# General code placed ahead of the main code, and 192-token tails stored in eight or nine transfers

## The chip, the core and the metric

The kernel runs on one core of a Trainium2 chip. The metric is the device time of one execution in microseconds (us). Times inside an execution are counted from the start of its profiled span. The profile names the engines PE (matrix products), DVE (vector), ACT (scalar), POOL (GpSimd) and SP (sync); the granted clock is the share of full clock speed that PE was allowed.

A run is called slow when it is over 1.5% above the fastest run of the same kernel.

## The reference, cut to what matters

```python
B, N, m, C = 4, 12480, 32, 128            # x: 4 x 12480 x 128, inducing: 32 x 128
def mab(q, kv):                            # attention of q over kv
    s = scale * (q @ kv.T); a = softmax(s); return a @ kv
h = mab(inducing, x)                       # per batch: 32 x 128
y = mab(x, h)                              # 4 x 12480 x 128
out = gelu(y @ w_in) @ w_out               # 128 -> 2048 -> 128, all float32 outside
```

Both inputs and outputs are large against the arithmetic: 25.6 MB of tokens are read and 25.6 MB are written. Each batch of 12480 tokens is cut into six units of 2048 tokens and a tail of 192. The kernel uses a short form of the second part that holds for small values, checks on the chip that it was allowed to, and otherwise runs a slow general code.

## The kernel before, where the change touches it

A pair of full units lies on 128 partitions and is stored in one transfer of 2 MB. The tail lies on 96 partitions with 1 KB each and is stored in one transfer of 96 KB. In the last batch each unit (1 MB) is stored alone. All stores, the first load and the inducing points are issued by the sync engine (SP); all other loads, which convert to 16 bits on the way, by GpSimd (POOL). Data is moved by 16 DMA engines, called rings here; a transfer is spread over up to 16 of them. The packet records do not name a ring, so "a ring ends" means one of the 16 last data packets, or completions, of a transfer.

```python
x_first = sb.tile([128, 32, 128], FP32, tag="o", bufs=OBUFS)
...
nc.sync.dma_start(out=x_first[:, :16, :], in_=src[:, :16, :])     # first unit, as fp32
nc.gpsimd.dma_start(out=x_pair[:, 16:, :], in_=src[:, 16:, :])    # bulk loads follow
a_load(units[0][2])
...
nc.sync.dma_start(out=ind_s, in_=inducing)                        # inducing points, 16 KB
nc.tensor.transpose(indT_ps, ind_s, identity[:M, :M])             # first work of PE
...
def b_store(bt, u, alone):
    if alone:
        c0, c1, o = u.c_pair, u.c_pair + u.nc, bt.live[("o", u.idx)]
    else:
        c0, c1, o = 0, u.held, bt.live[("pair", u.pair)]
    nc.sync.dma_start(out=u.rows_of(out)[:, c0:c1, :], in_=o)
...
with tc.If(flag > 0, preferred_fallthrough_block=False):
    general(tc, x, moe_w_in, moe_w_out, out, ind_s, identity)     # the rare code
```

The instructions of each engine are issued in the written order. Completion of a transfer is counted on a semaphore, which an engine can wait for. The framework gives SP's transfers eight of them in turn (108, 109 and 113 to 118 in the issue records), and lets SP wait, before it issues a transfer, until the transfer eight back, which had the same semaphore, has landed entirely.

## Time and profile before

| | before |
|---|---|
| time | 134.17 us median (134.0 to 134.32) |
| span of the profiled execution | 132.8 us |
| rings' busy share (sum of the four queues) | 98.4%, so 2.1 us idle (packets overlap, so some 3.7 us too low) |
| first load landed (its semaphore full) | 6.1 us |
| last arithmetic | 122.9 us |
| last store's data: median ring / last ring | 128.6 / 131.2 us |

First the page of the kernel before: its span, the rows of the DMA in 40 slices of 3.3 us (a digit is the busy share in tenths, the row below it GB/s), and the shares of the two data queues (packets, MB, share of the 16 engines' span). Queue 0 carries GpSimd's loads, queue 1 SP's transfers.

```profile
span 132.8 us, 3490 instructions
...
DMA  4999999999999999999999999999999999999970
GB/s 123 302 223 215 217 200 220 212 220 210 220 205 220 215 200 313 333 398 367 299 318 348 266 227 324 321 412 425 430 423 426 415 437 413 411 434 425 421 300 15
...
q0 software_dynamic: 2848, 13.30, 49.5%
q1 hardware_dynamic: 2800, 26.63, 48.3%
```

The DMA row is what matters: from the second slice to the 38th it never falls below 9. The kernel is limited by its transfers, and idle time of the arithmetic engines costs nothing as long as this row stays full.

Then how it starts: the timeline of SP, and the first instruction of PE, with the start in us, the duration, and in brackets how long the engine was idle before it and what ended that.

```profile
0.75 0.38 SPq L285 DMA_DIRECT2D x_first<-in_x_dram  x1
1.19 0.42 SPq L295 DMA_DIRECT2D ind_s<-in_inducing_dram  x1
```

Last, the waits of SP, by what ended them (us in total, number, longest):

```profile
SPq L713 <- DVE pair L701: 90.2, 9, 42.7
SPq L713 <- POOL pair L686: 8.6, 5, 2.1
SPq L713 <- DVE o L701: 8.6, 6, 3.0
SPq L1141 <- DMA out_dram<-o: 5.9, 3, 3.3
```

At the store line (L713) SP waits for results only, never for an earlier store. Its waits for stores are at the end of the program (L1141).

### The profile page before, as it was taken

Reading aid. Unit: us, or ns where it says so; the run is one execution under the profiler, and the core shown is the slowest. Engines: PE = TensorE matmul, PEld = TensorE weight load, DVE = VectorE, ACT = ScalarE, POOL = GpSimd, SP = SyncE. Lnnn points to the kernel's source line nnn. Section 1 sums busy time; section 2 is a strip of 40 time slices with the busy share of each in tenths; the row PEclk is TensorE's granted clock in tenths of the full one; section 3 lists DMA queues with packets and bytes.
Section 4 is the critical chain, followed back from the end, with each engine's and each line's share of the span. In section 5 each row is a group of like instructions: output and inputs, shape, how many; then the busy total and the mean of one; then the engine's idle time right before and its main releaser. Section 6 shows DMA issues by size and latency. Waiting matters only on the chain. (4 is left out here: it accounts for less than half of the span.)

```text
span 132.8 us, 3490 instructions
## 1 busy us (share of the span) xinstructions
PE 97.3 (73%) x1365; PEld 56.6 (43%) x1365; DVE 93.4 (70%) x266; ACT 76.2 (57%) x173; POOL 65.3 (49%) x85
## 2 busy tenths in 40 slices
PE   0098678449999999999697979957988779295000
PEld 0036545349465556665363555624544424131000
DVE  1086557323699998999999489749989999998000
ACT  3004273316866879598878458967779759174000
POOL 6920131119344646894824409914167999556000
PEclk9999999965899999999999999999999999955555
DMA  4999999999999999999999999999999999999970
GB/s 123 302 223 215 217 200 220 212 220 210 220 205 220 215 200 313 333 398 367 299 318 348 266 227 324 321 412 425 430 423 426 415 437 413 411 434 425 421 300 15
DMA packets 5666, 40.17 MB, mean 303 GB/s; under 512 B 624, under 2 KB 1936, under 8 KB 2192
## 3 DMA queue, kind: packets, MB, share of 16 engines
q0 software_dynamic: 2848, 13.30, 49.5%
q1 hardware_dynamic: 2800, 26.63, 48.3%
q8 instruction: 11, 0.18, 0.5%
q14 instruction: 7, 0.06, 0.1%
HBM read 27.67 MB, written 25.56 MB: 401 GB/s over the span
## 5 line engine op out<-in xcount | busy, mean ns | idle before, releaser
L686 POOL TENSOR_TENSOR pair<-pair,rr 128x512 f32<-128x512 f32 x29 | 30.3, 1056 | 29.1 <-ACT pair L355 19.9
L670 PE MATMUL at<-q,e 128*128 128x512 f16 (+1 forms) x104 | 33.5, 389 | 7.2 <-DVE o L701 2.4
L367 PE MATMUL tr<-identity_h,xh 128*128 128x128 f16 x392 | 29.3, 227 | 2.3 <-DMA xh<-in_x_dram 2.1
L701 DVE TENSOR_TENSOR pair<-at,rr 128x512 f32<-128x512 f32 x41 | 26.8, 679 | 3.1 <-DMA out_dram<-pair 1.6
L367 PEld LDWEIGHTS <-xh 128*128 128x128 f16 x392 | 24.5, 102 | 7.6 <-issue 3.5
L355 ACT ACTIVATE xT<-tr 128x1024 f16<-128x1024 f16 (+1 forms) x17 | 16.7, 981 | 19.1 <-PE tr L367 19.1
L353 DVE COPY xT<-tr 128x1024 f16<-128x1024 f16 (+1 forms) x35 | 21.9, 644 | 7.0 <-PE tr L367 6.7
L355 ACT ACTIVATE pair<-at 128x512 f32<-128x512 f32 x29 | 17.2, 598 | 3.1 <-PE at L670 1.7
L628 ACT ACTIVATE e<-s 128x512 f16<-128x512 f32 (+1 forms) x28 | 15.2, 563 | 6.4 <-PE s L616 5.2
L277 POOL DMA_DIRECT2D xh<-in_x_dram x15 | 8.3, 556 | 21.5 <-DMA xh<-in_x_dram 14.3
L393 ACT ACTIVATE e<-s 128x512 f16<-128x512 f32 (+1 forms) x28 | 15.2, 543 | 5.4 <-PE s L381 5.0
L670 PEld LDWEIGHTS <-e 128*128 128x128 f16 (+1 forms) x104 | 8.9, 105 | 11.5 <-issue 8.5
L415 PE MATMUL hun<-xh,e1t 128*32 128x128 f16 x392 | 10.5, 222 | 3.2 <-DVE e1t L407 3.0
L562 POOL TENSOR_TENSOR pt<-pt 128x512 f32<-128x512 f32 (+4 forms) x20 | 12.0, 601 | 1.5
L407 DVE STREAM_TRANSPOSE e1t<-e 128x256 int32<-128x256 int32 (+1 forms) x28 | 11.0, 399 | 2.2 <-ACT e L393 2.2
L381 PE MATMUL s<-xT,indT 128*32 128x512 f16 (+1 forms) x108 | 10.5, 376 | 1.6 <-ACT xT L355 0.8
L415 PEld LDWEIGHTS <-e1t 128*32 128x32 f16 x392 | 6.3, 96 | 11.5 <-DVE e1t L407 9.0
L701 DVE TENSOR_TENSOR o<-at,rr 128x512 f32<-128x512 f32 (+1 forms) x19 | 10.2, 558 | 0.9 <-PE at L670 0.7
L686 POOL TENSOR_TENSOR o<-o,rr 128x512 f32<-128x512 f32 x8 | 8.2, 1044 | 4.0 <-ACT o L355 2.3
L616 PE MATMUL s<-xT,hT 128*32 128x512 f16 (+1 forms) x100 | 9.7, 391 | 0.1
L640 PEld LDWEIGHTS <-e 128*128 128x128 f16 (+1 forms) x104 | 5.6, 99 | 5.0 <-issue 1.3
L640 PE MATMUL r<-strand,e 128*128 128x4 f16 (+1 forms) x104 | 6.9, 168 | 0.2 <-ACT e L393 0.2
(72 smaller groups left out, 93.0 us busy)
## 6 DMA issues: line engine op xcount, KB each, us to landing
out_dram<-pair SPq DMA_DIRECT2D x9, 2048.0 KB, 15.0
xh<-in_x_dram POOLq DMA_DIRECT2D x11, 1024.0 KB, 28.0
out_dram<-o SPq DMA_DIRECT2D x6, 1024.0 KB, 7.5
x_first<-in_x_dram SPq DMA_DIRECT2D x1, 1024.0 KB, 5.4
xh<-in_x_dram POOLq DMA_DIRECT2D x1, 512.0 KB, 7.3
w_in_h<-in_moe_w_in_dram POOLq DMA_DIRECT2D x1, 512.0 KB, 17.5
w_out_h<-in_moe_w_out_dram POOLq DMA_DIRECT2D x1, 512.0 KB, 19.5
out_dram<-o SPq DMA_DIRECT2D x4, 96.0 KB, 12.4
```

Of the source, the lines that this page charges most:

```text
L353: nc.vector.tensor_copy(out=out, in_=in_)
L355: nc.scalar.activation(out=out, in_=in_, func=AF.Copy)
L367: nc.tensor.transpose(tr[:, c - c0, : u.p], xh[: u.p, c, :], identity_h[: u.p, : u.p])
L393: nc.scalar.activation(out=e1[: u.p, : u.nc // 2, :, :], in_=s1[: u.p, : u.nc, :].rearrange("r (a b) i -> r a i b", b=2), func=AF.Exp, sca ...
L407: nc.vector.transpose(out=pairs(e1t)[: u.p, :n], in_=pairs(e1)[: u.p, :n])
L415: nc.tensor.matmul(bt.hun[32 * j : 32 * j + 32, :], e1t[: u.p, c // 2, :, c % 2], xh[: u.p, c, :], start=u.idx == 0 and c < 4, stop=c + 4 ...
L562: nc.gpsimd.tensor_tensor(out=bt.pt[:, :, :, :half], in0=bt.pt[:, :, :, :half], in1=bt.pt[:, :, :, half : 2 * half], op=ALU.add,)
L628: nc.scalar.activation(out=e2[: u.rows, : u.cols], in_=s2[: u.rows, : u.cols], func=AF.Exp, scale=SCALE,)
L640: nc.tensor.matmul(r2[: u.p, ci, : u.nj], e2[: u.rows, ci * u.p : (ci + 1) * u.p], strand[: u.rows, : u.nj], start=True, stop=True,)
L670: nc.tensor.matmul(at[: u.p, : u.nj, :], e2[: u.rows, ci * u.p : (ci + 1) * u.p], bt.q[: u.rows, : u.nj, :], start=True, stop=True,)
L686: nc.gpsimd.tensor_tensor(out=part, in0=part, in1=rr2[: u.p, ci, : u.nj].unsqueeze(2).broadcast_to([u.p, u.nj, 128]), op=ALU.mult,)
L701: nc.vector.tensor_tensor(out=ov[: u.p, ci, :, :], in0=at[: u.p, : u.nj, :], in1=rr2[: u.p, ci, : u.nj].unsqueeze(2).broadcast_to([u.p, u. ...
```

## The change

It has two parts. The stores of the tails are cut so that rings with a high number get fewer of the 96 rows: the rings do not end together, and one that ends late holds up the end. In the last batch, the parts are moved behind the last large store. And the rare code is laid ahead of the main code, so that the usual path does not jump over it at the end, where instruction fetches were seen among the last stores.

```diff
+    left_over = []
     def b_store(bt, u, alone):
         ...
-        nc.sync.dma_start(out=u.rows_of(out)[:, c0:c1, :], in_=o)
+        parts = [u.p]
+        if u.tail:
+            parts = [1, 3, 5, 7, 9, 11, 13, 15, 32]
+        if u.tail and u.b == B - 1:
+            parts = [2, 4, 6, 8, 10, 12, 14, 40]
+        left_over.append((u, parts, c0, c1, o))
+        if u.tail and u.b == B - 1:
+            return
+        for u, parts, c0, c1, o in left_over[::-1] if u.b == B - 1 else left_over:
+            p0 = 0
+            for n in parts:
+                nc.sync.dma_start(
+                    out=u.rows_of(out)[p0 : p0 + n, c0:c1, :], in_=o[p0 : p0 + n]
+                )
+                p0 += n
+        left_over.clear()
@@
+    nc.at_finalize(general_first)
     return nc
+
+def general_first(nc):
+    blocks = nc.main_func.blocks
+    rare = [b for b in blocks if "_true" in b.name]
+    rest = [b for b in blocks if "_true" not in b.name]
+    nc.main_func.blocks = rest[:1] + rare + rest[1:]
```

## The prediction

> **What bounds it now.** The DMA engines. The slice table shows the DMA row at 9 (90% or more) from the second slice to the 38th. The last load lands at 88.9 us; from then on only stores run, back to back. The last arithmetic ends at 122.9 us (timeline), the last store's final completion packet starts at 131.2 us, the span ends at 132.8. In the DMA packet records the 16 rings end the last store between 127.6 and 131.2 us, median 128.6. One ring is slow (8 KB about every 316 ns instead of 306), starts the last store 1.9 us behind, and also carries an 8 KB instruction fetch at 128.5 us, with a packet after it stretched to 0.82 us. Another gets a 16 KB fetch (0.89 us). These follow the branch over the general code.
>
> **What the change intends.** The Trainium skill ("DMA: Bandwidth & Descriptors", on why a DMA increments its semaphore by 16) says that a transfer issued from SP runs on the lowest-numbered k engines, k being the largest divisor of the partition count up to 16. Parts of 1, 3, ... 15 and 32 then put 10 rows on ring 0 and 2 on ring 15 instead of 6 each (no record here names rings). A row of 1 KB takes about 42 ns, so the last ring is spared 4 rows three times and 6 once: about 0.75 us. General code first removes the jump at the end and probably the late fetches: 0.4 to 0.9 us. Alone, these would give at most 1%.
>
> **What it adds.** 31 more transfers on SP, 0.33 to 0.41 us of issue each. Worse, the issue records show SP's transfers cycling through eight semaphores, and each reuse waits until the transfer eight back has landed. The tail is issued right behind a large store (61.2, 84.8, 106.4 us), so its eighth part waits for that store to land, and SP, in order, holds all later stores. The store queue drains at each tail:
> - Batch 0: loads still fill the rings; almost free.
> - Batches 1 and 2: no loads are left. About 0.5 us until SP sees the landing (as at the end now), two part issues 0.9, issue to first packet 1.0 (as for the first load): 2.5 us empty each. The next stores' data are ready (94.4, 111.4 us), so 5 us are lost.
> - Batch 3: the eighth part waits for the very last large store. Then come its issue, SP's flag load, branch and closing waits, about 2.7 us, hidden today: about 3 us.
>
> Sum: 8 lost, less 0.75 of rows, about 0.8 of fetches, and up to 1 because an empty queue lets the late ring catch up: +5.7 us.
>
> **Predicted: 140.0 us, range 136.7 to 142.3. Faster by over 2%: 0.04; within 2%: 0.14; slower: 0.82.**
>
> **What would show it.** SP waits at the store line for DMA out_dram, many us in total, none today. GB/s dips below 300 near slices 30 and 35. The next large stores issue only near 99 to 101 and 115 to 117 us. Tail stores land last, and SP's flag load comes after 134 us. The late fetch records are gone, and the start is longer by at most 0.3 us. Without these waits the end should come at 131.5 to 132.5 us.
>
> **What would make it wrong.** Semaphores assigned otherwise than in turn; a drain costing less because the late ring sets the pace anyway; a fetch at the start, when all engines jump over the general code, delaying the first loads by 1 to 2 us.

## More of the kernel before

The kernel before takes 134 to 135 us on the chips that were used.

```profile
6.43 0.28 PE L297 MATMUL indT_ps<-identity,ind_s 32*128 32x32 f32 x1 [6.43 <-DMA ind_s<-in_inducing_dram]
```

The first load is issued at once. It has the rings to itself until 4.7 us, and PE begins at 6.4 us, when the inducing points that follow it have landed.

## The result, and the profile after

The changed kernel takes 145.11 us (144.9 to 145.43) against 134.17 us. Ratios here are the mean time of one kernel's fast runs over that of the other's of the same rounds, so not quite the ratio of the medians that are quoted. This one is 1.082, with a 95% interval of 1.079 to 1.085. The results were correct. The direction was forecast, the size was not: +10.9 us instead of +5.7, outside the range.

The same parts of the page, after:

```profile
span 143.3 us, 3526 instructions
...
DMA  2999999999999999999999939999459996399990
GB/s 31 200 270 304 220 190 231 215 213 215 209 219 208 220 213 222 288 334 297 332 322 311 407 161 379 405 389 434 188 233 439 430 405 283 122 405 421 421 402 28
...
q0 software_dynamic: 2848, 13.30, 46.2%
q1 hardware_dynamic: 3042, 26.63, 45.0%
```

The four queues' shares now sum to 91.8% of 143.3 us, that is 131.5 us busy, against 98.4% of 132.8 us, 130.7 us. So the work of the rings is the same within 1 us, and their idle time grew from 2.1 to 11.8 us (both read low by some 3.7 us, since packets overlap; the growth of 9.7 is what counts). That is nearly the whole loss, and the digits show where it is: three holes, at slices 24, 29 to 30 and 34 to 35. The prediction had two. In the table of stretches (from:to, length, busy us of each engine, granted clock, DMA share, GB/s) the holes look like this:

```profile
core 0: us, PE busy (x) PEld busy (x) DVE busy (x) ACT busy (x) POOL busy (x), PEclk, DMA share, GB/s
...
84.00:86.00 2.00, 2.00 (x11) 0.94 (x11) 0.64 (x2) 1.33 (x3) 0.92 (x1) 1.00 0.12 47
...
102.00:104.00 2.00, 2.00 (x26) 1.06 (x23) 1.98 (x4) 1.50 (x3) 0.00 (x0) 1.00 0.16 49
104.00:106.00 2.00, 1.55 (x28) 0.76 (x28) 1.93 (x5) 1.96 (x6) 1.03 (x1) 1.00 0.41 155
...
121.00:123.00 2.00, 0.09 (x1) 0.00 (x0) 1.93 (x6) 0.63 (x2) 1.64 (x2) 1.00 0.09 30
123.00:125.00 2.00, 1.36 (x9) 0.85 (x9) 2.00 (x5) 0.18 (x1) 0.52 (x1) 0.74 0.33 118
```

The arithmetic engines go on working in most of these stretches; what the rings lacked is told by the waits of SP below. In the kernel before, the share in such stretches is 0.99 or more:

```profile
core 0: us, PE busy (x) PEld busy (x) DVE busy (x) ACT busy (x) POOL busy (x), PEclk, DMA share, GB/s
...
102.00:104.00 2.00, 1.55 (x27) 1.00 (x30) 1.79 (x5) 1.42 (x4) 2.00 (x3) 1.00 0.99 418
115.00:117.00 2.00, 1.75 (x11) 0.99 (x10) 1.89 (x7) 0.74 (x2) 1.00 (x1) 0.77 1.02 430
```

The waits of SP name the reason for the holes. There are now waits at the store line (L726) for large stores:

```profile
SPq L726 <- DVE pair L701: 71.5, 6, 48.7
SPq L726 <- DMA out_dram<-pair: 17.3, 4, 7.3
```

The hole at 121 us in full, from the issue and packet records of the trace (not a view of the profile):

```
issue   114.30  third pair of batch 2 (2 MB), waits for results
issue   114.72 .. 120.41  tail parts of 1, 3, 5, 7, 9, 11, 13 partitions
packets 120.64 .. 122.41  the 16 rings end the third pair (median 120.73)
issue   122.92  tail part of 15 partitions: waited for that pair
issue   123.29  tail part of 32 partitions
issue   123.79  next large store, without a wait for results
packets 124.63  its first packet
```

The rings stood still for 3.9 us (median ring to next packet). The holes at 84 and 103 us have the same form: 2.8 and 3.9 us.

What was not foreseen stands at the start:

```profile
1.22 2.80 SPq L285 DMA_DIRECT2D x_first<-in_x_dram  x1
4.07 0.53 SPq L295 DMA_DIRECT2D ind_s<-in_inducing_dram  x1
```

```profile
17.72 0.28 PE L297 MATMUL indT_ps<-identity,ind_s 32*128 32x32 f32 x1 [17.72 <-DMA ind_s<-in_inducing_dram]
```

The issue of the first load takes 2.80 us instead of 0.38. Its first packet moves at 7.4 us instead of 1.8, and it lands at 15.7 us instead of 6.1. PE begins 11.3 us later, and all arithmetic runs some 9 us late to the end: the flag's last instruction is at 131.3 us instead of 122.7.

```profile
131.29 0.14 DVE L980 TENSOR_SCALAR failed<-tot 1x1 int32<-1x1 f32 x1
```

```profile
122.73 0.14 DVE L963 TENSOR_SCALAR failed<-tot 1x1 int32<-1x1 f32 x1
```

(The first line is of the changed kernel, the second of the kernel before, both from the timeline.) The trace also shows instruction fetches of 8 and 16 KB at 1.8 to 2.0 us, which are not there before, while those of the last 5 us are gone. The Trainium skill ("Runtime: NRT & Kernel Launch", instruction fetch mechanics) says that a taken branch whose target is outside the prefetched window forces a fetch before execution goes on. The trace agrees in that the fetches follow the jump over the rare code; it does not show that SP's 2.8 us are that stall.

One part of the intent is met. All 16 rings now end the last large store between 139.7 and 140.0 us, against 127.6 to 131.2 us before. The rows are not shown to be the reason: the rings restart together after the hole at 121 us, and in `first3_parts` (below), whose last tail is whole, the completions of the four large stores after the last hole also lie within 0.4 us, until instruction fetches at 131.6 and 132.1 us hold one ring back by some 2 us. And the rule for the number of engines holds. The Trainium skill ("DMA: Bandwidth & Descriptors", why a DMA increments its semaphore by 16) says that a transfer issued from SP uses the largest k up to 16 that divides the partition count, and that each engine used posts one completion. Nine parts of 1 to 15 and 32 then post 80 completions, the last tail's eight parts 66 (40 partitions run on 10 engines). Three times 80 plus 66, less the 64 of four whole tails, is 242 more. The trace has 578 completion packets on SP's queue after and 336 before: 242 more.

### The profile page after: what moved, and what is told of

Same layout as the page of the kernel before. It is cut to its first block, busy times and chain, and to the rows that moved or that the text cites. A ratio compares the mean times of both kernels' runs of the same rounds, so it can differ in the third digit from the quotient of the medians.

```text
span 143.3 us, 3526 instructions
## 1 busy us (share of the span) xinstructions
PE 96.7 (67%) x1365; PEld 56.5 (39%) x1365; DVE 93.6 (65%) x266; ACT 76.0 (53%) x173; POOL 65.6 (46%) x85
## 5 line engine op out<-in xcount | busy, mean ns | idle before, releaser
L670 PEld LDWEIGHTS <-e 128*128 128x128 f16 (+1 forms) x104 | 8.9, 105 | 11.7 <-issue 8.7
## 6 DMA issues: line engine op xcount, KB each, us to landing
xh<-in_x_dram POOLq DMA_DIRECT2D x11, 1024.0 KB, 18.1
```

The costliest lines, as they stand in the source:

```text
L670: nc.tensor.matmul(at[: u.p, : u.nj, :], e2[: u.rows, ci * u.p : (ci + 1) * u.p], bt.q[: u.rows, : u.nj, :], start=True, stop=True,)
```

## The experiments

Two theories stood at the outset. **W**: the loss is from waits on the eight semaphores alone; late arithmetic is hidden, since the rings are the limit. **S**: the start is a second cost of its own.

### One part of the change at a time

`gf_only` has general code first and the tails whole (the second half of the diff alone). `parts_only` has the first half alone.

> General code first, tails stored whole as before. Theory S (start): the jump at the start makes the sync engine stall in the issue of the first fp32 load (2.8 us in the changed kernel, 0.38 before), that load then shares the rings with the bulk loads and lands about 15 us into the span instead of 5, all arithmetic runs about 9 us late, and the store stream at the end is starved. It expects the last arithmetic near 131 us instead of 122.9 and a time of 137 to 141 us. Rival W (only the semaphore waits of the many small stores cost; the rings are the limit, so late arithmetic is hidden): 133.5 to 135.5 us. Both expect no instruction fetch records in the last 5 us.

> Tails in nine and eight transfers, general code behind as before. Theory S: the start is as before (first load lands at 5 us), the tail of batch 0 is covered by loads, the store queue drains at the tails of batches 1 and 2 only, about 2.5 to 3.5 us each, and 2 to 3 us come at the end: 139.5 to 142 us. Rival W: the whole loss of 10.9 us is here, 144 to 146 us.

`gf_only` took 142.1 to 142.4 us in three runs and 139.6 in one. Since the three lie over 1.5% above the one, they count as slow. It was repeated with more runs:

> The general-code-first kernel once more, since its first job held one run at 139.6 and three near 142.2 us. Theory S expects both levels to lie 5 to 8 us above before, with the first load landing near 15 us and the inducing points (queued behind it) near 17 us in each; the rival, that the higher level was a disturbance of that job, expects all runs near 139.6 us.

`gf_again` took 139.5 to 141.3 us in four fast runs, and 142.1 and 142.7 in two slow ones: ratio of the fast runs 1.038 (1.032 to 1.044). The granted clock is 0.93 to 0.94 in the fast runs and 0.91 and 0.93 in the slow ones, so a lower clock does not clearly go with the higher level; what makes it is open. In both jobs the profiled run fell in the higher level. Its start is that of the changed kernel: the issue of the first load takes 2.9 us in `gf_only` (3.3 in `gf_again`), and PE begins at 18.1 us.

```profile
1.21 2.91 SPq L285 DMA_DIRECT2D x_first<-in_x_dram  x1
```

So W falls: even in the fast runs the order of the code alone costs about 5 us, although not one store was touched.

`parts_only` took 143.47 us, ratio 1.068 (1.064 to 1.072). Its start is as before (first load issued in 0.41 us, PE begins at 6.3 us). Its rows on the page show the forecast two holes and a longer end, and no hole at batch 0:

```profile
DMA  4999999999999999999999999997499990999940
GB/s 125 300 228 208 205 206 224 215 222 215 210 214 215 199 317 327 405 347 299 334 329 234 212 330 424 431 435 300 159 417 391 440 390 25 378 424 412 412 183 14
```

At +9.1 us it lies between the expectations of S (139.5 to 142 us) and of W (144 to 146 us). The two parts are not additive: 9.1 and about 5 make 10.9 together.

### Where the small transfers cost

`first3_parts` cuts only the tails of batches 0 to 2; `last_parts` only the last one, behind the last large store.

```diff
+        parts = [1, 3, 5, 7, 9, 11, 13, 15, 32] if u.tail and u.b < B - 1 else [u.p]   # first3_parts
+        if u.tail: parts = [u.p]                                                       # last_parts
+        if u.tail and u.b == B - 1: parts = [2, 4, 6, 8, 10, 12, 14, 40]
```

> Nine transfers for the tails of batches 0 to 2, the last tail whole and in its old place, general code behind. Theory of the semaphore waits: two drains of the store queue, about 2.5 us each, less up to 1 us because the late ring catches up: 137.5 to 139.5 us. If the small transfers as such cost nothing and the waits are hidden: 134 us.

> Only the last tail split, in eight transfers behind the last large store; the others whole; general code behind. Theory of the semaphore waits: the eighth part waits for the last large store, then its issue, the flag load and the closing waits follow: 136 to 137.5 us. Rival: no wait ends the kernel, and rows taken off the late ring gain 0.3 us: 133.8 us.

`first3_parts` took 141.17 us, ratio 1.050 (1.047 to 1.054): +6.8 us, above the 137.5 to 139.5 that were expected. `last_parts` took 136.65 us, ratio 1.016 (1.010 to 1.022): +2.2 us, as expected (clear of zero, though not of the 2% at which a run is called slower). Their sum, 9.0, is the 9.1 of `parts_only`.

The packet records of `first3_parts` say why the holes were undersized:

```profile
DMA  4999999999999999999999999999299994499991
```

From the last ring's end to the next store's first packet it took 2.2 us in both (99.62 to 101.84 and 118.39 to 120.59 us), a little less than the 2.5 of the prediction. But SP waits for the last of the 16 rings, and the other 15 had ended up to 1.7 us earlier: the median ring ended at 98.57 and 116.74 us, so it stood still for 3.3 and 3.9 us. Together that is 7.1 us, where the prediction had 5.0 and left this wait out. What it took off, up to 1 us because the late ring catches up, is there: the last large store's last completion comes 1.6 us behind the median one, where it was 2.5 us before.

### Is it the number of transfers, or the semaphore that comes round?

`six` and `seven` put the same rows on the same rings; `seven` only cuts the part of 48 partitions into 16 and 32. The code order and the last tail are as before.

```diff
+        parts = [3, 5, 11, 13, 16, 48] if u.tail and u.b < B - 1 else [u.p]        # six
+        parts = [3, 5, 11, 13, 16, 16, 32] if u.tail and u.b < B - 1 else [u.p]    # seven
```

> Tails of batches 0 to 2 in six transfers (3, 5, 11, 13, 16, 48 partitions), general code behind, last tail whole. Theory of the semaphore waits: with six small stores the next large store needs the semaphore of the large store before last, so the queue never drains: no waits of the sync engine for a large store at a tail, 133 to 135 us. Rival (small transfers cost in proportion to their number, by issue time or by per-transfer overhead): about 6/9 of the 6.8 us that nine transfers cost, so 138 to 139 us.

> The same rows per ring as six, but the 48-partition part cut into 16 and 32: seven transfers. Theory of the semaphore waits: the next large store now needs the semaphore of the large store right ahead of the tail, the queue drains at the tails of batches 1 and 2, 1.4 us from the landing to the next first packet on top of the wait for the slowest ring: 137.5 to 140 us, a step against six. Rival: one transfer more is worth a sixth of what six cost, under 1 us more than six.

`six` took 135.6 us, just above its expectation, ratio 1.002 (0.995 to 1.009); `seven` took 139.57 us, ratio 1.035 (1.029 to 1.041). The seventh transfer of each tail costs some 4 us (1.035 against 1.002), the five that `six` adds to the one whole transfer cost nothing that these runs can measure (at most 0.9%). The rows of DMA on the two pages, `six` first:

```profile
DMA  4999999999999999999999999999999799899993
```

```profile
DMA  4999999999999999999999999999679997599990
```

The holes at slices 29 to 30 and 34 to 35, of batches 1 and 2, are in the second only; at the 7 of `six` (slice 32) SP waited for results. With seven parts it is the next large store itself whose semaphore belongs to the large store ahead of the tail. In `six` SP does wait for large stores too, which was not expected, 14.3 us in two waits (`six` first, then `seven`):

```profile
SPq L716 <- DVE pair L701: 76.4, 7, 41.6
SPq L716 <- DMA out_dram<-pair: 14.3, 2, 9.4
```

```profile
SPq L716 <- DMA out_dram<-pair: 22.1, 5, 9.4
```

The two waits of `six` cost nothing: both are behind the tail of batch 0 (they end at 67.5 and 77.3 us), where loads and large stores are still in the queues. The wait is not the cost; the empty queue is.

One rival is ruled out at batch 1 only: that SP, busy with issuing parts, comes late with the next large store. In `seven` the parts of that tail were all issued by 94.8 us, 3.6 us before the median ring ended the large store ahead of them, so the wait alone made that hole. At batch 2 the issues were slower (up to 1.2 us each) and went on until 116.1 us, 0.4 us after the median ring had ended; there a part of the hole would have come without the wait.

### The start by itself

`late_first` leaves the code order and the stores of the kernel before, and only holds the first load back about 3 us, by a clearing of its buffer that it must follow. `gf_hoist` is `gf_only`, with SP's two loads issued in the entry block, ahead of the jump.

```diff
+    nc.vector.memset(x_first[:, :24, :], 0.0)                      # late_first
     nc.sync.dma_start(out=x_first[:, :16, :], in_=src[:, :16, :])
@@
     nc.main_func.blocks = rest[:1] + rare + rest[1:]
+    entry, body = rest[0].instructions, rest[1].instructions       # gf_hoist
+    early = [i for i in body if "SP" in str(i.engine) and "DMA" in type(i).__name__][:2]
+    for i in early:
+        body.remove(i)
+    at = [n for n, i in enumerate(entry) if "SP" in str(i.engine)][-1]
+    rest[0].instructions = entry[:at] + early + entry[at:]
+    rest[1].instructions = body
```

> The kernel before, its code order and its stores untouched; only the first fp32 load is held back about 3 us on the sync engine by a clearing of its buffer that it must follow. Theory S (a late first load meets the bulk loads on the rings, lands 10 us late, and all arithmetic with it): first load lands at about 15 us, last arithmetic near 131 us, 138 to 143 us, as with general code first. Rival: the general code first costs by something else (more instruction fetches, branches): at most 1 us more than before, so 134 to 135.5 us.

> General code first, but the two loads of the sync engine (first fp32 load and inducing points) are issued in the entry block, ahead of the jump; stores as before. Theory S: the first load lands at about 5 us again, the whole loss of general code first is gone, and the late fetches are missing from the end: 132.8 to 134.3 us. Rival (the jump costs by itself): 138 us or more.

`late_first` took 141.12 us, ratio 1.046 (1.040 to 1.052). Its timeline, SP and then PE (one line more in the source, so L286 is the old L285):

```profile
4.38 0.38 SPq L286 DMA_DIRECT2D x_first<-in_x_dram  x1
4.82 0.47 SPq L296 DMA_DIRECT2D ind_s<-in_inducing_dram  x1
```

```profile
18.47 0.28 PE L298 MATMUL indT_ps<-identity,ind_s 32*128 32x32 f32 x1 [18.47 <-DMA ind_s<-in_inducing_dram]
```

A load that is issued 3.6 us later lands 10 us later (16.4 instead of 6.1 us). Once GpSimd's bulk loads have begun, at 2.7 us, it has to share the rings with them. The Trainium skill ("DMA: Bandwidth & Descriptors", queues, rings and completion order) says that each engine goes round between the queues that have work for it, packet by packet. The trace of the changed kernel agrees in that both move at once, though not in equal parts: from 8.5 to 14.5 us SP's queue has 0.37 of the rings' time, the bulk loads 0.65. That the first packet moves only at 7.4 us (8.1 in `late_first`), over 3 us after its issue, suggests that work already queued goes first as well.

Why this costs, in a kernel whose rings are never idle at the start, is seen at the other end of `late_first`:

```profile
DMA  3999999999999999999999999977809599999993
GB/s 30 192 265 284 241 200 217 220 216 213 203 226 211 220 213 216 216 253 349 401 319 321 349 427 431 426 323 302 328 5 450 225 408 410 368 424 410 429 394 155
```

The loads ended early (80.7 us instead of 88.9); later there are no loads, the results come late, and the store queue runs empty three times between 94 and 112 us, for some 4 us at 101 us. Bytes that were moved early do not help when the ones that can be moved last depend on arithmetic.

`gf_hoist` took 135.32 us, ratio 1.006 (0.998 to 1.013). So nearly the whole cost of general code first lies in the place of these two loads, which S expected. But the gain that S also expected (132.8 to 134.3 us) did not come, though the late fetches are gone. PE still begins 2.5 us late, since the inducing points land at 8.8 us instead of 6.3:

```profile
8.92 0.28 PE L297 MATMUL indT_ps<-identity,ind_s 32*128 32x32 f32 x1 [8.92 <-DMA ind_s<-in_inducing_dram]
```

### Both together, and a version meant to win

`after_hoist` is the changed kernel with the two loads ahead of the jump (the edit of `gf_hoist` on top). `mended` keeps the intent and takes both costs away: loads ahead of the jump, inducing points loaded from the scalar engine so that they do not queue behind the first load, tails in six parts, the last tail in five and ahead of the last large store. `best` has the old code order, tails of 90 and 6 partitions (no row on the last ring), and the inducing points from the scalar engine.

```diff
-    nc.sync.dma_start(out=ind_s, in_=inducing)
+    nc.scalar.dma_start(out=ind_s, in_=inducing)                   # mended, best: ahead of x_first
@@
+        parts = [u.p]                                              # mended
+        if u.tail:
+            parts = [3, 5, 11, 13, 16, 48] if u.b < B - 1 else [2, 8, 12, 14, 60]
@@
+        parts = [90, 6] if u.tail else [u.p]                       # best
```

> The whole change, but with the sync engine's two first loads issued ahead of the jump. If start and semaphore waits are two separate costs that overlap in the changed kernel: the queue drains at two tails instead of three, and the time is that of the small transfers alone, 142 to 143.5 us (no late fetches at the end). If the start cost comes on top: 137.5 to 139 us, since about 6 us would go.

> Both costs taken away, the intent kept: general code first with the first loads ahead of the jump, the inducing points loaded from the scalar engine so that the tensor and vector engines do not wait for them behind the big load, tails in six transfers (batches 0 to 2) and five (last batch, ahead of the last large store). No drains, no late fetches, rings ending within 1 us of each other: 131.5 to 133.5 us, against about 134.3 before. If the intent is worth nothing: 134 us or more.

> The old code order, tails in two transfers of 90 and 6 partitions (six rows off the last ring each time, no eighth transfer), inducing points loaded from the scalar engine. If the late ring is the last one and sets the end, 0.5 to 1.2 us are gained: 132.8 to 133.8 us. If the late ring is another, or the late fetches set the end alone: 134 to 135 us.

`after_hoist` took 141.67 us, ratio 1.050 (1.044 to 1.055), just under its first expectation. The hole of batch 0 is gone (two holes left, at 98 to 102 and 117 to 121 us):

```profile
DMA  4999999999999999999999999999299994499990
```

So in the changed kernel the third hole is an effect of the start: with the stores 9 us late against the loads, the loads were over when the tail of batch 0 drained the store queue. It is also 1.8 us faster than `parts_only` in medians of different jobs (ratios 1.050 and 1.068). So where a wait for the last store ends the kernel, the missing late fetches do pay: in `parts_only` one ring falls some 1.9 us behind the median right after fetches of 8 and 16 KB at 128.9 and 129.4 us and is still 1.7 us behind at the last large store, in `after_hoist` there is no fetch and the spread of the completions stays at 0.2 us.

`mended` took 134.59 us, above its expectation of 131.5 to 133.5, ratio 0.996 (0.992 to 1.000); `best` 134.99 us, ratio 1.001 (0.995 to 1.006). In `mended` 15 rings end within 0.2 us of each other (130.3 to 130.4) and one at 131.2 us. The parts are not needed for that: in `gf_hoist`, with whole tails and no late fetch, the last completion also comes 0.7 us behind the median (1.0 in `mended`, 2.5 before). Even rings and no late fetch are thus worth 0.4% here, or 0.8% at the end of the interval. `best` shows no gain, and its trace says why: the last completion of the third-last large store, ahead of any late fetch, lies 2.0 us behind the median one, and that of the last store 2.5 us, against 1.8 and 2.5 us in the kernel before. So taking rows off the last-numbered ring did not relieve the late one; late fetches fall into the stretch in which the last half microsecond is added. No version was found that beats the kernel before.

## Why the prediction was wrong

- **"The store queue drains at each tail"**: right. `six` against `seven` shows that it is not the number of transfers but whose semaphore the next one needs, and the waits of SP name the large store.
- **"2.5 us empty each"**: undersized. The 2.5 us from landing to the next packet measured 2.2, but a term is missing: 15 rings wait for the last one, so the median ring stood still 3.3 and 3.9 us (`first3_parts`). The catching up of the late ring, "up to 1", was 0.9 us at the last large store. The first three tails were put at 5.0 - 1 us, less a share of the row gain, and measured 6.8. So the parts alone cost 9.1 us (`parts_only`), more than the 5.7 forecast for the whole change.
- **"Batch 3 ... about 3 us"**: right. `last_parts` is 2.2 us longer; from the last ring's data to the end of the span it takes 4.4 us instead of 1.6, so 2.8 us for the end itself, and the rings ended 0.6 us earlier.
- **"Batch 0: loads still fill the rings; almost free"**: right for the split tails alone (`parts_only` has no hole there), wrong for the whole change (2.8 us), because of the next point.
- **"The start is longer by at most 0.3 us"**: this is the step that failed. The sum had no term for it. Among the things that could make it wrong stood a fetch at the start that delays the first loads by 1 to 2 us, thought of as a shift of the whole. What counts is not the shift (the rings begin 1.0 us later) but the order: the one load that all arithmetic waits for lost its lead over the bulk loads, landed 9.6 us late, and cost about 5 us alone (`gf_again` 1.038, `late_first` 1.046) and some 4 us inside the change (1.082 against 1.050 in `after_hoist`). With the start repaired the change would take 1.050 times 134.17, about 140.8 us, close to the forecast 140.0. That closeness is partly luck: the holes were put too small, and so was the gain from the missing fetches (about 0.8 forecast; 1.068 against 1.050 is some 2.5 us).
- **"The late fetch records are gone"**, "0.75 of rows": the fetches went and the rings end together, but neither showed as time in a kernel without holes (`mended`). The gain from the rows supposed that the late ring is among those relieved; in `best` its lag did not shrink.

The chain is thus: `parts_only` 9.1 us (6.8 for three tails, 2.2 for the last), with the start repaired and the late fetches gone about 7 us (`after_hoist`), with the late start 10.9 us. What remains open is why SP's issue took 2.8 us after the jump, what makes the two levels of `gf_only`, and which ring is the late one.

## What to carry to other kernels

When transfers are cut into more pieces, count the completion semaphores: a piece that reuses that of the large transfer right ahead of it empties the queue, and the price is the restart plus the wait for the slowest of 16 rings. Where all work starts from one load, protect its lead over the bulk loads: a few us late at its issue can become ten at its landing, and they are paid at the end of the kernel, where stores then wait for arithmetic. And an engine's wait says nothing by itself: look whether the row of the bound resource has a hole at that time.

## What the Trainium skill lacked or had wrong

- "DMA: Bandwidth & Descriptors" treats the issue time as small and gives no figure for a loaded queue. In the changed kernel the issue of a transfer of 3 to 13 partitions took 0.26 to 0.34 us at the tail of batch 0, beside loads, but mostly 1.0 to 1.2 us at the tails of batches 1 to 3. A large store ahead is not enough to explain it: at the tail of batch 1 of `first3_parts` it took 0.27 to 0.33 us. What decides is open.
- No page has the cost of emptying a store queue: from the last ring's end to the next store's first packet 2.2 us with two small issues between (`first3_parts`), 1.4 to 1.6 us with none (`seven`).
- "Runtime: NRT & Kernel Launch" (instruction fetch mechanics) warns of a taken branch but gives no size. Here the issue of the first transfer behind the jump took 2.8 to 3.3 us instead of 0.38 (three traces). Its first packet came 3.4 us after that, but so it did without a jump (3.3 us in `late_first`).
- "DMA: Bandwidth & Descriptors" (queues, rings and completion order) has the turn-taking of queues, but not what it does to a load that comes second: 3.6 us later at the issue, 10 us later at the landing (`late_first`).
- The same page (latency and other measured facts) says that engines 7 and 15 are usually slower. The records name no engine; they show one ring at about 316 ns for 8 KB where the others take 306. Relieving the last-numbered ring of 24 rows gained nothing (`best`, 1.001) and left the late ring's lag at 2.5 us, so here the late one is not engine 15, if the numbering is as the page has it; engine 7 was not tested.
